# Segment 0 of a segmented memory attention: more projection work between the output rounds, output weights in smaller loads, value rows stored later

## The chip, the cores and the metric

The kernel runs on one core of a Trainium2 chip. The metric is the device time of one execution in microseconds (us), lower being better. A core has TensorE (PE in the profile; PEld is its weight load), VectorE (DVE), ScalarE (ACT), GpSimd (POOL) and SyncE (SP). DMA transfers are issued here from the queues of SP and ACT and run on the core's 16 DMA engines. "The profile" is one execution recorded by the hardware profiler; its page and the views of its trace are quoted below.

## What is computed

Two blocks follow each other on 2048 rows of 640 features. The first is attention with a recurrent memory: the rows are cut into 64 segments of 32, and each segment attends to itself and to 8 memory rows, which are the first 8 output rows of the segment before. The second is a dense layer with a squared ReLU.

```python
for s in range(n_seg):                         # 64 segments, one after another
    xs = x[:, s * seg_len:(s + 1) * seg_len, :]          # layernorm(x), 32 rows
    h = concatenate([mem, xs], axis=1)                   # 8 + 32 rows
    q = einsum('btd,dhe->bhte', h, Wq)                   # 32 heads of 128
    k = einsum('btd,dhe->bhte', h, Wk)
    v = einsum('btd,dhe->bhte', h, Wv)
    scores = where(mask, einsum('bhqe,bhke->bhqk', q, k) * scale, -1e9)
    o = einsum('bhqk,bhke->bhqe', softmax(scores), v)
    o = einsum('bhte,hed->btd', o, Wo)
    mem = o[:, :M, :]                                    # needed by the next segment
    outs.append(o[:, M:, :])
h = x + concatenate(outs)
out = h + relu(layernorm(h) @ w1 + b1)**2 @ w2 + b2
```

## The kernel before

Every matmul, transposes included, is issued by a helper, so all of them stand at line 114 or 118 of the profile; they are told apart by the tiles they write and read. The order of all instructions on all engines is written out by hand (`tc.manual_schedule`): each engine, and each DMA queue, works through its instructions in the order in which the Python code issues them, and waits in place where an operand or a buffer is not ready.

**Blocks and segments.** Four segments make a block of 128 rows; there are 16 blocks. A segment works on 32 rows: the 8 memory rows and the first 24 of its own rows. The last 8 rows of each segment do not touch the memory, so their q, k and v ("tails") are computed ahead, for a whole block at a time, as `tail_units`. A unit is four matmuls of 32 x 512 that run side by side in four column groups of the array; five units make one half (16 heads, 512 columns on 128 partitions) of a block's q, k or v. `tail_quarters` makes a quarter with matmuls 256 wide. Such units are put into the list `fill`, and `run(fill, n)` issues the next n of them at chosen places of `step`, the code of one segment.

**A segment (`step`).** q and k are projected; their results are copied out by ACT into row tiles (a pool of four buffers) and turned by DVE into qT and kT. Scores, softmax, v (copied by ACT into the tile v, lines 590 and 611), the products with the values (tile po) and 16 output rounds (`wo_rounds`, tile pw) follow. A round multiplies two heads of oT with wo in four matmuls of 320 columns. Rounds 0 to 7 use the even heads and rounds 8 to 15 the odd heads: round 8 the heads 1 and 17, round 9 the heads 3 and 19, round 12 the heads 9 and 25, and so on. After the last round DVE and ACT turn the 8 new memory rows into hT (`mem_to_hT`, lines 294 to 297), which the next segment's q needs. Fill issued behind the last round runs meanwhile.

**Segment 0** is special: its q, k and v are made in `start`, while the weights stream in (wv, wq, wk, then wo), together with those of block 0's tails. Its call of `step` has `ready` set.

**Values of the tails.** The value rows of a block's tails lie in row order; the product needs them in another order. So they are stored to a buffer in DRAM (vt_d, line 363) and gathered back into vt4 (`tails_v_in`, four DMAs, line 417). For block 0 the two stores are issued from ACT's queue in `start`; the gather for segment 0 (rows of which every fourth is used) comes from ACT's queue, and that for segments 1 to 3 from SP's queue, before the k stream. For blocks 1 and up the rows are kept in SBUF space that is not needed yet ("parked": parts of hnT0, ht0, oTts, vt4s, hT4, the tile v of segment 1, an xn tile) and stored in batches at the start of segments 1, 2 and 3 (`soon`, `stores`, last kept first). When no parked space is left, a row tile is used and stored at once.

**Loads on SP.** `load_wo` loads wo in eight DMAs: two of eight heads (the even heads), then odd heads in loads of 4, 4, 2, 2, 2 and 2 heads. Behind them stand the load of x for block 1 (line 139), the four gathers and, in segment 0, four loads of tail rows (line 148).

**Instruction padding.** PE's instructions are counted (`issued`), and `align` splits some 512-wide projections of the q and k of a segment into two of 256 (`halved`), so that the count at a chosen place of the segment falls on a multiple of 256.

Of the kernel before, what the change touches and what calls it, by code (L numbers as in the profile page):

```python
# [12 lines left out]
BF16 = mybir.dt.bfloat16  # L13
# [3 lines left out]
def kernel(  # L17
# [16 lines left out]
    nc = tc.nc  # L34
    _, S, D = A_x.shape
# [70 lines left out]

    ctx.enter_context(tc.manual_schedule(engines=None))

    issued, halved = [0], [0]
    BLOCK, AHEAD, PLACE = 256, 65, 34  # L110

    def matmul(*a, **k):
# [45 lines left out]

    def load_wo():
        wov = A_Wo.rearrange("h e d -> e h d")  # L160
        for h0, k in ((0, 8), (16, 8), (1, 4), (17, 4), (9, 2), (25, 2), (13, 2), (29, 2)):
            hs = slice(h0, h0 + 2 * k - 1, 2)
            nc.sync.dma_start(out=wo[:, hs, :], in_=wov[:, hs, :])  # L163

# [63 lines left out]
    def proj(w, by, lhs, n, ps, c0, c1):  # L228

        if by == "columns":  # L230
            wr = w[:].rearrange("p (c g j n k e) -> p c n k g j e", c=DC, g=G, n=2, j=4, k=4)
        elif by == "half":
            wr = w[:].rearrange("p (c k j n e) -> p c n k j e", c=DC, k=G, n=2, j=4)
        else:
            wr = w[:].rearrange("p (c k n f) -> p c n k f", c=DC, k=G, n=2)
        for c in range(c0, c1):
            for k in range(4):
                r = slice(32 * k, 32 * k + 32)
                if c and by == "columns" and halved[0]:
                    halved[0] -= 1  # L240
                    for u in range(2):
                        matmul(ps[r, u * 256:(u + 1) * 256], lhsT=lhs(c), rhs=wr[:, c, n, k, u * 2:u * 2 + 2],
                               start=False, stop=(c == DC - 1 and u == 1))
                    continue
                matmul(ps[r, :], lhsT=lhs(c), rhs=wr[:, c, n, k], start=(c == 0), stop=(c == DC - 1))

    def mmtile():
        return mm.tile([128, 512], F32, tag="mm", name="ps")
# [103 lines left out]
        return [unit(cs) for cs in ((0, 1), (2, 3), (4,))]  # L352

    def tail_out(b, which, n, ps):
        kept = which == "v" and 0 < b and len(parked) > 0
        row = parked.pop(0)() if kept else spare.pop(0) if spare else rowtile()[:]
        if which == "v" and b == 2:
            nc.vector.tensor_copy(out=row, in_=ps)
        else:
            evac_row(which, row, ps)  # L360
        if which == "v":
            def store(eng=nc.sync):
                eng.dma_start(out=vt_d[b, 2 * n:2 * n + 2].rearrange("j r f -> r j f"),
                              in_=row.rearrange("r (j f) -> r j f", j=2))
            if kept:
                stores.append(store)
            else:
                store(nc.sync if b else nc.scalar)
            return
        if n == 0:  # L370
            tails.setdefault(b, {})[which] = s2.tile([128, H, 32], BF16, tag=which + "Tt", name=which + "Tt")
        dst = tails[b][which]
        late.append(lambda: flip(row, dst, n))
# [30 lines left out]
        if "k" in which:  # L404
            nc.gpsimd.tensor_copy(out=kT[:, h0:h1, SEG:NK], in_=k)

    vt4s, stores = {}, []
    vt_d = dram.tile([NB, 4, 128, 2 * E], BF16)

    def tails_v_in(b, eng, s0=0, s1=4):  # L410
# [49 lines left out]
    def step(b, sp, v=None):  # L460
# [178 lines left out]
        wo_rounds(main, pw, 6, 8)  # L639
        if ready:  # L640
            tokens_sum()
        run(fill, 2 if ready else 1)
        wo_rounds(main, pw, 8, 12)
        if ready:
            run(fill, len(fill) - 6)
        wo_rounds(main, pw, 12, 16)

        if not ready:
            tokens_sum()
# [27 lines left out]
            tails_in((s + 1) // 4, (s + 1) % 4)  # L677
        run(mid, 2)
        o = wo_out(pw)
        run(fill, 100)  # L680
        if s > 1:
            store_main(o, s - 2)
        if last:
# [107 lines left out]
    def start():  # L791

        v = s2.tile([128, EG], BF16, tag="v", name="v")
        vs.append(s2.tile([128, EG], BF16, tag="v", name="v"))
        hT4s[1] = s2.tile([128, DC, 4, SEG], BF16, tag="hT4", name="hT4")
        park(hT4s[1][:, 0:4].rearrange("p c s t -> p (c s t)"))
        for u in range(2):
            park(vs[0][:, 512 * u:512 * u + 512])
        parked.append(lambda: s1.tile([128, D], BF16, tag="xn", name="vrow")[:, 0:512])
        main = lambda c: hT4s[0][:, c, 0, :]  # L800
        units = []

        def stream(which, w, dst, k=0):
            pa = pop.tile([128, 4, 512], F32, tag="po", name="pa")
            for c in range(DC):
                if which == "v" and c == DC - 1:
                    run(units, k)
                for n in range(2):
                    proj(w, "half" if which == "v" else "columns", main, n, pa[:, n, :], c, c + 1)
                for n in range(2):  # L810
                    proj(w, "order" if which == "v" else "columns", lambda c: tail_rows(0, c), n, pa[:, 2 + n, :], c, c + 1)
                if c < DC - 1:
                    run(units, k)
                    run(late, 100)
                if which == "q" and c == 1:
                    ln_stats(("t", 2))
                    ln_norm(("t", 2))
            for n in range(2):
                if which == "v":
                    nc.scalar.copy(out=v[:, n * 512:(n + 1) * 512], in_=pa[:, n, :])  # L820
                else:
                    row = rowtile()[:]
                    evac_row(which, row, pa[:, n, :])
                    flip(row, dst, n)
                    tail_out(0, which, n, pa[:, 2 + n, :])
                    late.pop()()
                    tails_in(0, 0, which, n * 16, (n + 1) * 16)
            if which == "v":
                for n in range(2):
                    tail_out(0, which, n, pa[:, 2 + n, :])  # L830

        ahead = [tail_units(1, "v"), tail_units(2, "v", (mmtile, lambda: chn.tile([128, 512], F32, tag="ch", name="pc")))]
        units += [a[n * DC + c] for c in range(DC) for a in ahead for n in range(2)]
        stream("v", wv, None, 4)
        ln_stats(("t", 1))
        ln_norm(("t", 1))
        units += tail_units(3, "v")
        units.insert(8, lambda: ln_transpose(("t", 1))())
        units.insert(11, lambda: None)
        units.insert(12, lambda: None)  # L840
        for b in (4, 5, 6):
            units += tail_units(b, "v")
        run(units, 6)
        load_tail_rows(2)
        load_w(wk, A_Wk)
        load_wo()
        load_x(1)
        stream("q", wq, qT, 7)
        for n in range(2):
            spread(n)  # L850
        units.append(lambda: ln_transpose(("t", 2))())
        units += tail_units(7, "v") + tail_units(1, "q") + tail_units(8, "v")
        run(units, 15)
        tails_v_in(0, nc.scalar, 0, 1)
        tails_v_in(0, nc.sync, 1, 4)
        stream("k", wk, kT, 6)
        units += tail_units(1, "k")
        run(units, 100)
        return v
# [13 lines left out]
    for b in (9, 10, 11, 12):  # L873
        parts = tail_units(b, "v")
        halves += [parts[:DC], parts[DC:]]
    del halves[-1], halves[4]
    quarters = [(11, "v", 0, 0), (11, "v", 0, 1)] + [(12, "v", 1, u) for u in range(2)]
    quarters += [(b, "v", n, u) for b in range(13, NB) for n in range(2) for u in range(2)]
    for b in range(NB):
        for sp in range(4):  # L880
            run(soon, 1)
            if sp == 2 and b + 2 < NB:
                load_x(b + 2)
            if b == 0:
                for h in range((3, 1, 1, 1)[sp]):
                    fill += halves.pop(0)
                if sp:
                    fill += tail_quarters(*quarters.pop(0))
                if sp < 3:
                    soon.append(lambda n=(8, 5, 5)[sp]: [stores.pop()() for _ in range(min(len(stores), n))])  # L890
                if sp == 1:
                    late.append(lambda: ln_stats(("t", 3)))
                    mid.append(lambda: ln_norm(("t", 3)))
                if sp == 2:
                    ln_turn(("t", 3))
                    late.append(lambda: ln_stats(1))
                    mid.append(lambda: ln_norm(1))
                if sp == 3:
                    ln_turn(1)
                    spare += [hnT0[:, c, :] for c in range(2)]  # L900
            elif b < NB - 1:
                if sp == 0:
                    fill += tail_units(b + 1, "q")[0:DC] + tail_quarters(b + 1, "q", 1, 0)
                if sp == 1:
                    parts = tail_units(b + 1, "k")
                    fill += tail_quarters(b + 1, "q", 1, 1) + parts[0:DC]
                if sp == 2:
                    fill += parts[DC:]
                    if quarters:
                        fill += tail_quarters(*quarters.pop(0))  # L910
# [141 lines left out]
```

## Time and profile before

| | |
|---|---|
| Time, median of 3 runs | 952.49 us (950.98 to 954.1) |
| The profiled execution | 952.75 us |
| Its span, first to last instruction | 950.9 us |
| TensorE busy | 927.1 us (97%), 25883 matmuls |
| VectorE, ScalarE, GpSimd busy | 704.2 us (74%), 546.0 us (57%), 256.7 us (27%) |
| DMA | 56.74 MB; the 16 engines are busy about all the time up to 60 us, and 10% of it or less in the long middle |
| Mean granted clock of TensorE | 0.998 |
| Chain that ended last | PE 92%, DMA 3%, DVE 2% |
| Segment 0 | about 49.8 to 63 us; a segment of block 0 after it takes about 11.8 us |

A share of busy time is a mean over stages with different limits. The first 60 us are the stage in which the weights come in; the middle is 63 segments in a chain; the dense block is the end. The change is at the border of the first stage and the second, so the table's shares say little of it, and the views that follow look at 50 to 70 us.

### The profile page before, as it was taken

To read this page: it belongs to the slowest core of one execution; us is meant where nothing else is said; L and a number is where in the kernel's file an instruction comes from. 1 tells how busy PE (TensorE), PEld (TensorE's weight loads), DVE (VectorE), ACT (ScalarE), POOL (GpSimd) and SP (SyncE) were. 2 spreads that over 40 slices of the span, in tenths; PEclk is the share of its full clock that TensorE was granted. 3 is DMA by queue.
4 is the path that set the end of the run, shared out by engine and by line. 5 is a ranking of instruction groups with operands and counts; after the bars stand their busy time and mean duration, and the time that the engine had idled before them with its cause. 6 is when DMAs were issued, how large, how long until landed. Compare 5 with 4: busy or idle time off the path is not lost.

```text
span 950.9 us, 57556 instructions
## 1 busy us (share of the span) xinstructions
PE 927.1 (97%) x25883; PEld 571.7 (60%) x25883; DVE 704.2 (74%) x2136; ACT 546.0 (57%) x1342; POOL 256.7 (27%) x798
## 2 busy tenths in 40 slices
PE   6989999999999999999999999999999998999998
PEld 2555665676566656666666566666666555555555
DVE  3268888888888888888888888888788888566632
ACT  3546666666666666666666666666566655523321
POOL 1012222222222222222222222222222233254200
PEclk9999999999999999999999999999999999999999
DMA  9973200101010101010101010101010111643220
GB/s 359 399 245 91 45 24 20 24 19 24 19 24 14 29 13 31 12 32 9 34 9 35 8 34 9 35 9 32 10 33 11 52 43 21 208 105 90 90 56 29
DMA packets 60710, 56.74 MB, mean 60 GB/s; under 512 B 27560, under 2 KB 56624, under 8 KB 58544
## 3 DMA queue, kind: packets, MB, share of 16 engines
q1 hardware_dynamic: 59776, 52.74, 18.5%
q8 instruction: 202, 3.31, 1.5%
q14 instruction: 44, 0.36, 0.1%
q10 hardware_dynamic: 688, 0.33, 0.1%
HBM read 38.37 MB, written 9.44 MB: 50 GB/s over the span
## 4 chain that ended last, share of the span: by engine, by line
PE 92%; DMA 3%; DVE 2%; ACT 1%; SPq 1%; issue 1%; POOL 0%; ACTq 0%; DVEq 0%
PE ps L114 62%; PE pw L114 16%; PE y L114 6%; PE po L114 5%; DMA vt_d<-row 1%; PE sm L114 1%; DMA wo<-in_A_Wo_dram 1%; SPq L163 1%; DMA vt<-vt_d 1%; PE pa L114 1%; DVE wk L975 0%; DVE lnst L170 0%; DMA xt<-in_A_x_dram 0%; ACT otc L295 0%; DVE otr L294 0%
## 5 line engine op out<-in xcount | busy, mean ns | idle before, releaser
L114 PEld LDWEIGHTS <-hT 128*32 128x32 bf16 x8358 | 220.3, 96 | 134.0 <-DVE hT L297 9.3
L114 PE MATMUL pw<-wo,oT 128*32 128x320 bf16 x4224 | 180.3, 301 | 3.5 <-DMA wo<-in_A_Wo_dram 3.2
L114 PE MATMUL ps<-wv,hT 128*32 128x512 bf16 x2520 | 177.4, 380 | 0.0
L114 PE MATMUL ps<-wq,hT 128*32 128x512 bf16 (+1 forms) x3143 | 160.2, 338 | 3.8 <-DVE hT L297 3.8
L114 PE MATMUL ps<-wk,hT 128*32 128x512 bf16 (+1 forms) x2575 | 159.2, 375 | 0.1
L114 PEld LDWEIGHTS <-oT 128*32 128x32 bf16 x4224 | 97.5, 96 | 58.5 <-DVE oT L252 20.2
L655 POOL TENSOR_TENSOR pkt<-ek,rk 128x64 bf16<-128x64 bf16 x64 | 19.2, 300 | 413.4 <-DVE rk L653 413.4
L261 ACT ACTIVATE row<-ps 128x512 bf16<-128x512 f32 (+1 forms) x170 | 94.0, 562 | 15.3 <-PE ps L114 11.9
L266 DVE STREAM_TRANSPOSE qT<-row 128x512 bf16<-128x512 bf16 x128 | 89.9, 702 | 9.7 <-ACT row L261 5.6
L974 ACT ACTIVATE wv<-ps,b1f 128x512 bf16<-128x512 f32 (+1 forms) x56 | 37.5, 672 | 67.4 <-PE ps L114 66.5
L443 ACT CAST oT<-po 128x512 bf16<-128x512 f32 x128 | 74.8, 587 | 0.0
L295 ACT COPY otc<-otr 64x40 f32<-64x40 f32 x126 | 28.0, 223 | 68.5 <-DVE otr L294 68.0
L454 POOL COPY qz<-qT 128x96 bf16<-128x96 bf16 x126 | 33.3, 265 | 115.4 <-DVE mx L505 58.2
L114 PEld LDWEIGHTS <-hTt 128*32 128x32 bf16 x1660 | 46.2, 98 | 29.8 <-issue 1.8
L114 PE MATMUL y<-wq,wk 128*128 128x320 bf16 x448 | 61.2, 300 | 0.2 <-DVE wk L975 0.2
L114 PEld LDWEIGHTS <-v 32*128 32x128 bf16 x4064 | 42.0, 91 | 32.0 <-issue 17.6
L263 ACT CAST row<-ps 128x512 bf16<-128x512 f32 (+1 forms) x111 | 60.2, 558 | 1.7 <-PE ps L114 0.9
L629 DVE TENSOR_REDUCE zk<-ek 128x8 f32<-128x320 bf16 x64 | 31.1, 486 | 38.1 <-ACT ek L628 38.1
L486 ACT CAST row<-ps 128x256 bf16<-128x256 f32 x126 | 40.7, 375 | 30.9 <-PE ps L114 30.9
L611 ACT CAST v<-ps 128x512 bf16<-128x512 f32 x63 | 36.9, 585 | 29.9 <-PE ps L114 29.9
L266 DVE STREAM_TRANSPOSE kT<-row 128x512 bf16<-128x512 bf16 x65 | 45.8, 705 | 10.1 <-ACT row L263 6.5
L114 PEld LDWEIGHTS <-wk 128*128 128x128 bf16 x448 | 40.5, 97 | 20.4 <-issue 5.0
(113 smaller groups left out, 1623.2 us busy)
## 6 DMA issues: line engine op xcount, KB each, us to landing
wv<-in_A_Wv_dram SPq DMA_DIRECT2D x5, 1024.0 KB
wq<-in_A_Wq_dram SPq DMA_DIRECT2D x5, 1024.0 KB
wk<-in_A_Wk_dram SPq DMA_DIRECT2D x5, 1024.0 KB
vt<-vt_d SPq DMA_DIRECT2D x60, 64.0 KB
xt<-in_A_x_dram SPq DMA_DIRECT2D x18, 160.0 KB
wo<-in_A_Wo_dram SPq DMA_DIRECT2D x2, 1280.0 KB
wq<-in_B_w_dram SPq DMA_DIRECT2D x1, 2080.0 KB
o_all<-o SPq DMA_DIRECT2D x128, 15.0 KB
```

The lines of the kernel that those rows point to most:

```text
L114: nc.tensor.matmul(*a, **k)
L261: nc.scalar.mul(out=row, in_=ps, mul=scale)
L263: nc.scalar.copy(out=row, in_=ps)
L266: nc.vector.transpose(out=dst[:, n * 16:(n + 1) * 16, 0:32], in_=row.rearrange("p (h e) -> p h e", e=32))
L295: nc.scalar.copy(out=tc_[:, a], in_=tr[64:128, a, :, 0:M])
L443: nc.scalar.copy(out=oTg[:, n, :, :, M:NK], in_=po[:, :, n * 128:(n + 1) * 128].rearrange("p g (j q) -> p g j q", q=32))
L454: nc.gpsimd.tensor_copy(out=d.rearrange("p a (j f) -> p a j f", j=3)[:, :, :, 0:M], in_=src[:, :, 0:3, :])
L486: nc.scalar.copy(out=row[:, u * 256:(u + 1) * 256], in_=ps[:, u * 256:(u + 1) * 256])
L611: nc.scalar.copy(out=v[:, 512:1024], in_=ps1[:])
L629: nc.vector.tensor_reduce(out=zk[:], in_=ek[:], op=ALU.add, axis=AX.X)
L655: nc.gpsimd.tensor_tensor(out=pkt[:], in0=ek[:, :, SEG:NK], in1=rk[:].unsqueeze(2).to_broadcast([128, HG, TL]), op=ALU.mult)
L974: nc.scalar.activation(out=r[:, 0:w], in_=ps[:, 0:w], func=ACT.Relu, bias=b1f[:, fc:fc + 1], scale=1.0)
```

## The change

- In segment 0 `fill` holds five halves, 25 units, instead of three halves, 15 units. The rounds 8 to 13 are issued in pairs, with 3, 5 and 4 units behind the pairs; 6 units remain behind the last round, with every matmul but those of the first chunk split in two (`split`).
- The odd heads of wo are loaded two at a time, in the order in which the rounds use them. There are ten loads of wo.
- Of block 0's value rows, every fourth is stored in `start` from ACT's queue, which is all that segment 0's gather reads. The rows themselves stay in parked space (one more xt tile is parked), and the full store is issued from SP's queue in segment 0, behind rounds 12 and 13 and their fill. The gather for segments 1 to 3 and the load of x for block 1 follow there; they stood in `start` before.
- The two halves that moved into segment 0 were four quarters in later segments: one in each of segments 1, 2 and 3, and one that makes the list of quarters one block shorter, so that block 13 has none.

```diff
-    issued, halved = [0], [0]
+    issued, halved, split = [0], [0], [False]
...
-        for h0, k in ((0, 8), (16, 8), (1, 4), (17, 4), (9, 2), (25, 2), (13, 2), (29, 2)):
+        for h0, k in ((0, 8), (16, 8), (1, 2), (17, 2), (5, 2), (21, 2), (9, 2), (25, 2), (13, 2), (29, 2)):
...
-                if c and by == "columns" and halved[0]:
-                    halved[0] -= 1
+                rhs = wr[:, c, n, k]
+                if c and (split[0] or by == "columns" and halved[0]):
+                    halved[0] -= 0 if split[0] else 1
+                    f = rhs.shape[1] // 2
                     for u in range(2):
-                        matmul(ps[r, u * 256:(u + 1) * 256], lhsT=lhs(c), rhs=wr[:, c, n, k, u * 2:u * 2 + 2],
+                        matmul(ps[r, u * 256:(u + 1) * 256], lhsT=lhs(c), rhs=rhs[:, u * f:(u + 1) * f],
...
-        kept = which == "v" and 0 < b and len(parked) > 0
+        kept = which == "v" and len(parked) > 0
...
-            if kept:
+            if b == 0:
+                first.append(store)
+                nc.scalar.dma_start(out=vt_d[0, 2 * n:2 * n + 2].rearrange("j (r s) f -> s r j f", s=4)[0],
+                                    in_=row[0:128:4].rearrange("r (j f) -> r j f", j=2))
+            elif kept:
                 stores.append(store)
             else:
-                store(nc.sync if b else nc.scalar)
+                store()
...
-        run(fill, 2 if ready else 1)
-        wo_rounds(main, pw, 8, 12)
-        if ready:
-            run(fill, len(fill) - 6)
-        wo_rounds(main, pw, 12, 16)
+            for h, k in ((8, 3), (10, 5), (12, 4)):
+                wo_rounds(main, pw, h, h + 2)
+                run(fill, k)
+            for f in first:
+                f()
+            tails_v_in(0, nc.sync, 1, 4)
+            load_x(1)
+        else:
+            run(fill, 1)
+            wo_rounds(main, pw, 8, 14)
+        wo_rounds(main, pw, 14, 16)
...
         o = wo_out(pw)
+        split[0] = ready
         run(fill, 100)
+        split[0] = False
...
+        parked.append(lambda: s2.tile([128, D], BF16, tag="xt", name="vrow")[:, 0:512])
...
         load_wo()
-        load_x(1)
...
         tails_v_in(0, nc.scalar, 0, 1)
-        tails_v_in(0, nc.sync, 1, 4)
...
-    del halves[-1], halves[4]
-    quarters = [(11, "v", 0, 0), (11, "v", 0, 1)] + [(12, "v", 1, u) for u in range(2)]
-    quarters += [(b, "v", n, u) for b in range(13, NB) for n in range(2) for u in range(2)]
+    quarters = [(b, "v", n, u) for b in range(13, NB) for n in range(2) for u in range(2)]
...
-                for h in range((3, 1, 1, 1)[sp]):
+                for h in range((5, 1, 1, 1)[sp]):
                     fill += halves.pop(0)
-                if sp:
-                    fill += tail_quarters(*quarters.pop(0))
```

More of the change, by code (lines that the diff above doesn't have):

```diff
@@ L238, in proj @@
                 r = slice(32 * k, 32 * k + 32)
-                if c and by == "columns" and halved[0]:
-                    halved[0] -= 1
+                rhs = wr[:, c, n, k]
+                if c and (split[0] or by == "columns" and halved[0]):
+                    halved[0] -= 0 if split[0] else 1
+                    f = rhs.shape[1] // 2
                     for u in range(2):
-                        matmul(ps[r, u * 256:(u + 1) * 256], lhsT=lhs(c), rhs=wr[:, c, n, k, u * 2:u * 2 + 2],
+                        matmul(ps[r, u * 256:(u + 1) * 256], lhsT=lhs(c), rhs=rhs[:, u * f:(u + 1) * f],
                                start=False, stop=(c == DC - 1 and u == 1))
                     continue
-                matmul(ps[r, :], lhsT=lhs(c), rhs=wr[:, c, n, k], start=(c == 0), stop=(c == DC - 1))
+                matmul(ps[r, :], lhsT=lhs(c), rhs=rhs, start=(c == 0), stop=(c == DC - 1))
     def mmtile():
@@ L405, in tails_in @@
             nc.gpsimd.tensor_copy(out=kT[:, h0:h1, SEG:NK], in_=k)
-    vt4s, stores = {}, []
+    vt4s, stores, first = {}, [], []
     vt_d = dram.tile([NB, 4, 128, 2 * E], BF16)
```

## The prediction

> **What bounds the kernel now.** The page first: TensorE is busy 97% of the span, and its share of the chain that ended last is 92%, so work taken from TensorE shortens the kernel one for one where TensorE is busy. The waits of TensorE came next: 3.2 us of its idle time, in 5 pieces, ends on the output weights (wo). The timeline of TensorE puts all five into segment 0 (columns: start, length, engine, line, operation, and in brackets the idle time before and what ended it):
>
> ```profile
> 54.99 0.32 PE L114 MATMUL pw<-wo,oT 128*32 128x320 bf16 x2
> 56.78 0.72 PE L114 MATMUL pw<-wo,oT 128*32 128x320 bf16 x14 [1.48 <-DMA wo<-in_A_Wo_dram]
> 57.68 0.31 PE L114 MATMUL pw<-wo,oT 128*32 128x320 bf16 x2 [0.18 <-DMA wo<-in_A_Wo_dram]
> 58.54 0.45 PE L114 MATMUL pw<-wo,oT 128*32 128x320 bf16 x6 [0.55 <-DMA wo<-in_A_Wo_dram]
> 59.39 0.31 PE L114 MATMUL pw<-wo,oT 128*32 128x320 bf16 x2 [0.40 <-DMA wo<-in_A_Wo_dram]
> 60.33 0.53 PE L114 MATMUL pw<-wo,oT 128*32 128x320 bf16 x6 [0.62 <-DMA wo<-in_A_Wo_dram]
> 60.48 2.94 PE L114 MATMUL ps<-wv,hTt 128*32 128x512 bf16 x24
> 62.95 1.89 PE L114 MATMUL ps<-wq,hT 128*32 128x512 bf16 x20
> ```
>
> The reader should see that rounds 8 to 15 wait for one load after another, and that the last six fill units (24 matmuls) only come behind them. The windows view, cut at the clock's steps, gives TensorE's busy time (first number after the length) and the granted clock (third number from the end):
>
> ```profile
> 53.74:57.15 3.41, 1.94 (x60) 1.09 (x55) 2.81 (x6) 0.73 (x2) 0.00 (x0) 1.00 1.07 363
> 57.15:60.56 3.41, 1.66 (x28) 0.54 (x23) 0.08 (x1) 0.00 (x0) 0.00 (x0) 1.00 0.77 258
> 60.56:63.97 3.41, 3.41 (x40) 2.76 (x35) 1.82 (x7) 1.97 (x5) 1.57 (x4) 0.50 0.22 73
> ```
>
> So a stretch with 1.66 us of work was followed by 3.41 us at half clock. The chain of waits shows the last load landing at 51.69 + 8.60 = 60.29. The last two views are the timelines of SP's queue and of ACT:
>
> ```profile
> 38.13 14.42 SPq L163 DMA_DIRECT2D wo<-in_A_Wo_dram  x8
> 52.65 0.74 SPq L139 DMA_DIRECT2D xt<-in_A_x_dram  x1
> 53.43 4.83 SPq L417 DMA_DIRECT2D vt<-vt_d  x4
> 58.56 3.12 SPq L148 DMA_DIRECT2D ht<-in_A_x_dram  x4
> 64.06 0.37 SPq L363 DMA_DIRECT2D vt_d<-row  x1
> 64.48 0.47 SPq L363 DMA_DIRECT2D vt_d<-vrow  x1
> 64.99 1.03 SPq L363 DMA_DIRECT2D vt_d<-v  x2
> 96.03 2.67 SPq L417 DMA_DIRECT2D vt<-vt_d  x4
> ```
>
> ```profile
> 69.39 0.58 ACT L590 CAST v<-ps 128x512 bf16<-128x512 f32 x1 [0.18 <-PE ps L114]
> ```
>
> The loads at lines 417 and 148 start as earlier wo loads land: a transfer is issued only when the eighth before it has landed, since eight semaphores go round. The two stores from v landed at 67.00 and 67.53 by the trace's completion events, and the copy at 69.39, which overwrites the same buffer, waited only for TensorE.
>
> **Step 1: the last output weight.** Three quarters of block 0's two value stores leave the stretch before it, 196,608 bytes. By bytes at the 415 GB/s of 10 to 20 us this is 0.47 us. By landings: the four weight chunks around the stores took from 26.67 to 38.11, 11.44 us, where an undisturbed chunk took 2.48 (38.11 to 40.59) and the row load among them 0.39 by its bytes; the rest is 1.1 us, three quarters of it 0.85. I take 0.8, as the landings hold the cost of 512-byte runs. Two-head loads in order of use don't change the last byte: an 8-head load took 3.58 us (49.49 to 53.07), a 2-head load 0.86 to 0.93. The last load lands at 60.3 - 0.8 = 59.5, earlier ones 0.9 apart: 58.6, 57.7, 56.8, 55.9. The two extra issues on SP are hidden by that backlog; without it they would cost some 0.5 us each.
>
> **Step 2: fill among the rounds.** Twenty 512-wide matmuls take 1.08 us (65.62 to 66.70), so a unit of four is 0.216. Ahead of the last round stood 9 units and now stand 19; the extra ten are 2.16 us inside waits of 3.23 us, which hide them. The last round again ends 0.58 after the last load, at 60.1. The next segment needs hT, ready 1.10 after that round (61.96 against 60.86), so at 61.2. The six units behind the round take 1.3 us from 59.7 at full clock, as the stretch before is now filled, and are done by 61.0. Segment 1 starts at 61.2, not 62.95: 1.75 us. Before, another 1.02 us of it ran at half clock, worth 0.51. Together 2.26 us ahead.
>
> **Step 3: what leaves later segments.** Four groups of twenty 256-wide matmuls are gone, one each in segments 1, 2, 3 and in block 13. The matmuls from 73.97 to 75.38 are sixteen wide and twenty narrow: 1.41 - 16 x 0.054 = 0.55 each, 2.2 us in all, TensorE being busy there. Another 168 matmuls are split in two (20 in segment 0 by the flag, and by the padding 128 in segments 1 to 4 and 20 in block 13). Two halves take 2 x 0.0275 against 0.054, so the cost is between nothing and 168 x 1 ns = 0.2 us; I take nothing, as the narrow ones stream without a gap in that row.
>
> **Step 4: a new wait in segment 1.** On SP now stand, in order: ten wo loads, four tail-row loads, two row stores, block 0's two full stores, the four gathers, x(1), two row stores, two parked rows, then v's second and first half. By the round of eight, block 0's second full store waits for the last wo load, so it is issued at 59.5. Alone a store lands in 1.9 us (64.06 to 65.93). Behind four row loads (0.21 each, landings 62.98 to 63.61) and three stores (0.53 each, their spacing), with its own 0.53, it lands in up to 3.0. I take 2.5, nearer the backlog: 62.0. The first gather waits for it. Four gathers take 2.7 us of issue (96.03 to 98.70), x(1) 0.55, five stores 0.53 each: v's first half is issued at 62.0 + 2.7 + 0.55 + 2.65 = 67.9 and lands 2.0 later, at 69.9. ACT's copy of segment 1's values into v must wait for that. TensorE would want it by 69.39 - 2.26 = 67.1. The copy takes 0.58, and the value matmuls behind it, at 70.17 before, start at 70.5. On ACT the second exponential is queued behind the copy, on TensorE everything, so the delay is carried on: the 2.26 us are gone and 0.35 more. Bounds of this link: landing at 69.2 to 70.4 by the store's 1.9 to 3.0, and later by 1.6 if the v store takes 3.6, as the one issued at 67.14 did (landed 70.72).
>
> The gathers, moved past the tail rows and stores, land about 66.1; values want them at 67.9, so 1.8 us hide them. x(1), moved the same way, lands near 67 and is read in segment 2, past 82. ACT keeps its two issues of block 0, smaller ones; POOL's queue issues no DMA here and is not touched. Block 12's rows are now read by fill near 96, and their transpose landed at 84.6.
>
> **Sum.** Profiled execution 952.75 = span 950.9 and 1.85 outside it; the median of runs is 952.49, 0.26 less. 952.75 - 2.2 + 0.35 = **950.9**. Its own range, by the bounds of step 4, is 950.2 to 953.0.
>
> **Rivals.** *The chain on SP is short enough.* If v's store lands by 67.1, segment 0's gain stays: 952.75 - 2.2 - 2.26 = 948.3. For it: issue and transfer overlap, and the fast DMA engines finish wo 2 us before the slow ones (landings 58.25 to 60.28). Against: the gathers wait for all engines. By the Trainium skill (DMA: Bandwidth & Descriptors, SWDGE vs HWDGE vs iDMA), a sequencer's time to initiate a transfer is usually small beside the transfer; by that rule this case would hold. The rows here disagree: 0.53 us of issue for each 128 KB store.
>
> *The clock falls in the new stall.* TensorE would stand from 67.9 to 70.5. A window of 3.41 us that holds 2.6 us of it has 0.8 us of work, less than the 1.66 that brought half clock; windows run free of the kernel, so about half of their positions hold enough. Price 3.41 / 2 = 1.7: 952.6. By the Trainium skill (TensorE: Matmul & The Clock Gate, What's actually happening) the clock drops after a whole idle window; by that this stall is too short, and the first case stays. The row at 57.15 dropped with half a window of work, so I keep this case.
>
> *Slower: a lagging DMA engine on both links.* Stores issued at 67.14, 67.67 and 68.21 landed 3.58, 3.25 and 3.03 us later, in place of 2.0. If block 0's store and v's store both meet that, 1.6 us each, the copy starts at 73.1 and values at 73.7, 3.55 us late, and a stall of 5.8 us holds a whole window, so the half clock is sure: 952.75 - 2.2 + 3.55 + 1.7 = 955.8. It decides from a v landing past 72.9. Against it: a lag hits three stores in nine.
>
> **How the numbers follow.** Forecast 0.42, short chain 0.24, clock 0.18, lag 0.16. The range takes in the first three: 948.0 to 953.8, and leaves the lag, 0.16, outside. A measurement of this kernel can tell about 0.3% (2.9 us) from no change. Faster by more is the short chain and the best end of the forecast, 0.25; slower by more the lag and a little, 0.18; within it 0.57.
>
> **What would show it.** Right: wo waits of TensorE under 1 us and its last round done near 60.1; clock 1.00 from 60 to 64; a TensorE gap of some 2.6 us in segment 1 ended by ACT's copy of v (line 596 now), that copy idle until a store from v lands near 69.9; segments 1 to 3 0.55 shorter each. Wrong: no such gap (then 948.3), or half clock near 70 to 74 (then 952.6 or more), or a last wo load still at 60.3.

## The result and the profile after

| | changed kernel | kernel before, same chip | ratio, 95% interval |
|---|---|---|---|
| time, median | 955.77 us (953.60 to 958.57, 12 runs) | 953.08 us (949.88 to 954.80, 12 runs) | 1.0032 (1.0021 to 1.0044) |
| profiled execution | 954.77 us, span 953.0 | 952.75 us, span 950.9 | |

The changed kernel is slower by about 0.3%; the forecast was 950.9 us, faster than before by 1.85. The views that follow answer to those of the prediction.

First the chain of waits in segment 1 (start, length, what). SPq is SP's queue, and line 365 is the store to vt_d.

```profile
68.37 0.53 SPq L365
...
68.94 3.26 DMA vt_d<-v
...
72.27 0.59 ACT v L596
...
72.91 0.32 PE po L114 x15
```

The last store from v is issued at 68.94 and lands 3.26 us later. ACT's copy into v waits for that, and the value products on TensorE wait for the copy. The timelines of ACT and TensorE say the same from their sides:

```profile
72.27 0.58 ACT L596 CAST v<-ps 128x512 bf16<-128x512 f32 x1 [4.36 <-DMA vt_d<-v]
72.75 0.30 ACT L514 ACTIVATE em<-sm,mx 128x40 bf16<-128x40 f32 x1
```

```profile
60.65 0.45 PE L114 MATMUL pw<-wo,oT 128*32 128x320 bf16 x6 [0.41 <-DMA wo<-in_A_Wo_dram]
60.80 1.60 PE L114 MATMUL ps<-wv,hTt 128*32 128x256 bf16 x44
62.25 1.27 PE L114 MATMUL ps<-wq,hT 128*32 128x512 bf16 x36
...
68.56 0.41 PE L114 MATMUL ps<-wv,hT 128*32 128x512 bf16 x4
72.91 0.27 PE L114 MATMUL po<-pTm,v 32*128 32x8 bf16 x16 [3.94 <-ACT v L596]
```

TensorE stands for 3.94 us where it did not stand before. The upper three lines are the end of segment 0: the output rounds are done just behind 60.65, and segment 1 starts at 62.25, not at 61.2 as predicted. SP's queue shows why v's stores come so late:

```profile
61.15 0.46 SPq L365 DMA_DIRECT2D vt_d<-ht  x1
63.16 2.63 SPq L423 DMA_DIRECT2D vt<-vt_d  x4
65.83 0.45 SPq L139 DMA_DIRECT2D xt<-in_A_x_dram  x1
66.39 0.88 SPq L365 DMA_DIRECT2D vt_d<-row  x2
67.31 1.01 SPq L365 DMA_DIRECT2D vt_d<-vrow  x2
68.37 1.65 SPq L365 DMA_DIRECT2D vt_d<-v  x2
```

The line at 61.15 is block 0's second full store. The gathers (line 423) wait until it has landed, and everything below stands behind them. Last the windows view at the steps of the clock (busy TensorE after the length; granted clock third from the end):

```profile
67.68:71.09 3.41, 1.30 (x52) 0.69 (x44) 1.15 (x7) 0.23 (x2) 0.00 (x0) 1.00 0.83 238
71.09:74.50 3.41, 1.59 (x36) 0.79 (x40) 1.14 (x6) 1.11 (x4) 0.00 (x0) 0.50 0.56 158
74.50:77.92 3.42, 3.42 (x104) 1.96 (x100) 1.70 (x4) 0.98 (x3) 0.00 (x0) 0.50 0.02 5
77.92:81.33 3.41, 3.10 (x84) 1.94 (x80) 2.30 (x9) 1.45 (x4) 0.99 (x3) 1.00 0.02 5
```

The half clock that stood at 60.56 before is gone from segment 0, but two windows of it now follow the new stall. From segment 1's first scores to segment 2's the kernel takes 17.75 us, where it took 11.91.

### The profile page after: what moved, and what is told of

It reads as the page before. It is cut to its first block, busy times and chain, and to the rows that moved or that the text cites. A ratio compares the mean times of both kernels' runs of the same rounds, so it can differ in the third digit from the quotient of the medians.

```text
span 953.0 us, 57809 instructions
## 1 busy us (share of the span) xinstructions
PE 927.1 (97%) x26002; PEld 570.4 (60%) x26011; DVE 700.8 (74%) x2136; ACT 545.3 (57%) x1340; POOL 257.2 (27%) x798
## 4 chain that ended last, share of the span: by engine, by line
PE 91%; DMA 6%; DVE 1%; ACT 1%; issue 0%; SPq 0%; DVEq 0%; ACTq 0%
PE ps L114 62%; PE pw L114 16%; PE y L114 6%; PE po L114 5%; DMA wo<-in_A_Wo_dram 2%; DMA wq<-in_A_Wq_dram 2%; DMA wk<-in_A_Wk_dram 1%; PE sm L114 1%; DMA wv<-in_A_Wv_dram 1%; ACT otc L297 0%; DMA vt_d<-v 0%; DVE otr L296 0%; DVE hT L299 0%; SPq L365 0%; DVE qT L268 0%
## 5 line engine op out<-in xcount | busy, mean ns | idle before, releaser
L114 PE MATMUL pw<-wo,oT 128*32 128x320 bf16 x4224 | 182.3, 302 | 1.6 <-DMA wo<-in_A_Wo_dram 1.3
L114 PE MATMUL ps<-wq,hT 128*32 128x256 bf16 (+1 forms) x3211 | 159.6, 333 | 5.0 <-DVE hT L299 5.0
L297 ACT COPY otc<-otr 64x40 f32<-64x40 f32 x126 | 28.0, 223 | 67.2 <-DVE otr L296 66.7
```

What stands on the lines that cost most here:

```text
L114: nc.tensor.matmul(*a, **k)
L297: nc.scalar.copy(out=tc_[:, a], in_=tr[64:128, a, :, 0:M])
```

## The experiments

Each run lies beside runs of the kernel before on the same chip. In the first group these had a median of 951.17 us, in the second (f) 949.31, in the third (g1 to g4) 952.58, so ratios are compared, not times. The main question is whether v's place in SP's queue is the cause, and what the rest of the change does.

**v's stores first (e1).** The changed kernel with the two stores of v ahead of block 0's full stores; nothing else is different.

```diff
-            for f in first:
+            for f in [stores.pop(-3), stores.pop(-3)] + first:
...
-                    soon.append(lambda n=(8, 5, 5)[sp]: [stores.pop()() for _ in range(min(len(stores), n))])
+                    soon.append(lambda n=(6, 5, 5)[sp]: [stores.pop()() for _ in range(min(len(stores), n))])
```

> The changed kernel, with the two rows parked in v stored on SP ahead of block 0's full stores, so that they land near 63 us and not at 72. Theory (ACT's copy into v waits for v's store, which stands behind the gathers on SP): the 3.94 us gap of TensorE in segment 1 is gone, the clock stays 1.00 from 60 to 80 us, the step from the scores of segment 1 to those of segment 2 falls from 17.75 to about 12.0 us, and the time to 950.0 (955.8 - 5.8) or 951.9 (953.1 less the 1.16 us by which segment 1 began earlier). Rival (the gathers are late, v only looks guilty): they are issued a little later still, so a gap over 2 us stays, now ended by a gather, and the time stays over 954. Rival (the time is lost after segment 1, by thin fill and splits): the time stays over 954 without a gap.

Measured: 950.21 us, ratio 0.9994 (0.9984 to 1.0005). In its timelines of SP's queue and of ACT the stores go out at 60.38, and the copy waits only for TensorE:

```profile
60.38 1.53 SPq L365 DMA_DIRECT2D vt_d<-v  x2
```

```profile
68.63 0.59 ACT L596 CAST v<-ps 128x512 bf16<-128x512 f32 x1 [0.22 <-PE ps L114]
```

There is no half clock, and the step from segment 1 to 2 is 11.89 us. So the place of these two stores makes the difference between slower and level. The gathers go out 1.3 us later than in the changed kernel, at 64.49, and land by 69.51. The last of the value products that read them starts at 69.56: no wait for them shows, but no room is left either.

**The fill part alone (e2) and the store part alone (e3, and again as g3).** e2 has the change's fill, rounds and wo loads, with stores, gathers and x(1) of before; e3 has the fill, rounds and wo loads of before, with block 0's full stores, gathers and x(1) issued ahead of rounds 14 and 15.

```diff
 e2, against the changed kernel
-        kept = which == "v" and len(parked) > 0
+        kept = which == "v" and 0 < b and len(parked) > 0
...
-            for f in first:
-                f()
-            tails_v_in(0, nc.sync, 1, 4)
-            load_x(1)
...
 e3, against the kernel before
-        wo_rounds(main, pw, 12, 16)
+        wo_rounds(main, pw, 12, 14)
+        if ready:
+            for f in first:
+                f()
+            tails_v_in(0, nc.sync, 1, 4)
+            load_x(1)
+        wo_rounds(main, pw, 14, 16)
```

> The changed kernel's fill, rounds and wo loads, with block 0's full stores, the gathers and the load of x where they stood before the change. Theory: no gap on v, since v's stores are issued near 64 as before the change; time 951 to 952. If the smaller stores of block 0 ahead of wo paid their 0.65 us, the last wo load lands 0.65 later here than in the run with v's rows first; if not, they are equal within 0.3. Rival (the fill between the rounds or the split matmuls lose the time): 955 or more.

> The kernel before with the store part of the change alone: every fourth row of block 0 stored early, full stores, gathers and x behind round 13 on SP, 15 fill units as before. Theory: ACT's copy into v waits until about 72 us, TensorE stands some 2 us in segment 1 and the clock halves behind it: 956 to 958. Rival (the fill is to blame): 953.

> The store part alone on the fill of before, again. Its first profile held the stall (3.71 us) and two windows of half clock, and was 4.5 us behind the first profile of before over segments 2 to 10, while its median was no slower. Theory (the stall is always there, and the rest of that kernel saved the instruction stalls that the profile of before had): gap of 3.4 to 4 us again, segments 11 to the last 597 to 599 us, median within 0.3% of before. Rival (stall in some executions only): a gap under 2.5 us in this profile, or a median 0.3% or more slower now.

Measured: e2 949.81 us, 0.9987 (0.9975 to 0.9998). e3 951.48 us, 1.0006 (0.9995 to 1.0016), and again 954.40 us, 1.0017 (1.0005 to 1.0030). The fill part alone is a small gain: 10 of its 11 runs have a mean clock of 1.000, where 28 of the 29 runs of before beside it lie below that. Its last wo load lands at 61.51, where e1's lands at 61.10; the 0.41 between them lies between the two cases of the expectation, so it doesn't settle whether the smaller stores save anything (step 1 below). The store part alone has the stall in both profiles, 3.71 and 2.12 us:

```profile
72.47 0.27 PE L114 MATMUL po<-pTm,v 32*128 32x8 bf16 x16 [3.71 <-ACT v L594]
```

Both runs missed their expectations: e3 was to take 956 to 958 us, or 953 by its rival, and g3 was to have a gap of 3.4 to 4 us again. The cost in the medians is under 2 us, against a stall of 2 to 4, and the parts do not add up to the whole (-0.13% and +0.06 or +0.17%, against +0.32 and, below, +0.45%). Where the rest of e3's stall is won back was not found. Stalls of TensorE with no wait shown, in segments 11 to 61, move by up to 4 us from one execution to the next (e3 597.62 us for that stretch, g3 601.75), so its profiles can't tell.

**TensorE kept busy (e4, f2).** 128 matmuls whose result nothing reads, ahead of segment 1's first value products: in e4 into a tile of its own, in f2 into columns 320 to 511 of po.

```diff
 f2 (e4: idle[r, 0:256] of idle = mmtile(), rhs=wv[:, 0:256])
+        if s == 1:
+            for i in range(128):
+                r = slice(32 * (i % 4), 32 * (i % 4) + 32)
+                matmul(po[r, i % 4, 320:512], lhsT=lhs(0), rhs=wv[:, 0:192], start=True, stop=True)
```

> The changed kernel, with 128 matmuls of 256 columns ahead of segment 1's first value products; nothing reads their result. They are 3.4 us of work inside the stall of 3.94. Theory (half clock behind the stall is worth some 1.9 us of the 5.84): the copy of v still waits until about 72, the clock stays 1.00, time 953.9. Rival (half clock costs nothing there, as other engines set the pace): 955.8.

e4 priced nothing: its tile took over the buffer that the copy into v reads, so the matmuls waited for the copy and ran behind it; 958.16 us, 1.0069 (1.0055 to 1.0083).

> The changed kernel unchanged, on the chip and in the minutes of the other experiments, with a second profile. Theory (the stall before ACT's copy into v is in every execution, some 3 to 4 us, and one or two windows of half clock follow, 1.7 us each): 954.5 to 957 where the kernel before is at 951 to 952, and the second profile shows a TensorE gap over 3 us on that copy again. Rival (the long landing of v's store is an accident of some executions, so that only part of the loss is always there): a gap of 2.0 to 2.6 us in the second profile, no half clock or one window, and a median of 952.5 to 954.

> The changed kernel with 128 matmuls 192 columns wide (2.6 us of TensorE at full clock) into columns of segment 1's po that nothing reads, ahead of that segment's first value products, so that TensorE works through the stall; unlike in the run before they share no buffer with what the copy into v reads. Theory (half clock follows from the idle time and costs half of what it covers): the value products start no later than in the changed kernel (72.9 give or take 0.5), the clock stays at 1.00 from 68 to 80, and the step from segment 1's scores to segment 2's falls from 17.75 to 15.7 to 16.1; the median lies 1.5 to 2 us under the changed kernel's. Rival (half clock comes from something else, or hides behind another wait): half clock at 71 to 78 stays, or the step stays within 0.5 us of 17.75.

Measured: the changed kernel again (f1) 953.21 us, 1.0045 (1.0033 to 1.0058), with a gap of 3.62 us and half clock from 71.25 to 78.08, much as in its first profile. f2 951.91 us, 1.0031 (1.0020 to 1.0043). f2's timeline, and its windows at the clock's steps:

```profile
68.37 1.67 PE L114 MATMUL po<-wv,hT 128*32 128x192 bf16 x72
70.30 1.34 PE L114 MATMUL po<-wv,hT 128*32 128x192 bf16 x56 [0.26 <-issue]
72.31 0.26 PE L114 MATMUL po<-pTm,v 32*128 32x8 bf16 x16 [0.67 <-ACT v L596]
```

```profile
67.86:71.28 3.42, 3.16 (x164) 2.85 (x156) 0.59 (x4) 0.00 (x0) 0.00 (x0) 1.00 0.67 195
71.28:74.69 3.41, 2.74 (x140) 1.68 (x132) 1.87 (x8) 1.46 (x4) 0.00 (x0) 1.00 0.48 136
```

The value products start at 72.31 with or without the idle matmuls (f1: 72.34), the clock stays full, and the step to segment 2 is 15.61 us where f1 has 17.79. So the half clock costs 2.2 us in a profile, and 1.3 us between the medians.

**v's stores three places earlier (g4).** Right behind x(1), ahead of two row stores and two parked rows, but still behind block 0's stores and the gathers.

```diff
             load_x(1)
+            for u in range(2):
+                stores.pop(-3)()
...
-                    soon.append(lambda n=(8, 5, 5)[sp]: [stores.pop()() for _ in range(min(len(stores), n))])
+                    soon.append(lambda n=(6, 5, 5)[sp]: [stores.pop()() for _ in range(min(len(stores), n))])
```

> The changed kernel, with v's two stores issued right behind x(1), ahead of the two row stores and the two parked rows (three places of the queue earlier than in the changed kernel, still behind block 0's stores and the gathers). Theory (the wait is the place of v's stores in SP's queue, and the packet of instructions at 67.7 to 68.7 on top): issued near 65.9 and 66.4, they are nearly down when the packet comes, land at 67.9 to 68.6, and the gap before the value products is 0 to 0.6 us, with no half clock; median 949.5 to 951 where the kernel before is at 949.3 to 951.2. Rival (the gathers in front hold the engines, whatever the place): landing past 69.5, gap over 1.2 us and a median 951 or more.

Measured: 954.35 us, 1.0021 (1.0011 to 1.0031). The theory missed, the rival held. Chain of waits:

```profile
66.98 4.39 DMA vt_d<-v
...
71.44 0.59 ACT v L596
...
72.08 0.30 PE po L114 x20
```

Issued 1.96 us earlier than in the changed kernel, the last store lands only 0.83 earlier. The first of the two takes 2.95 us, where a store takes 2.0. The load x(1) ahead of it takes 3.06 and the last gather 3.02, half a microsecond more than the 2.50 and 2.62 that they took in e3. So what stands in front of v's stores holds them up as well, as the rival had it; the rest of the 4.39 is the next point.

**The packets of instructions (g2, h1).** In the trace's packet records the instructions come as packets of 16,384 bytes, which in this stretch hold one DMA engine for 0.9 to 1.8 us each. One came at 68.67 in the changed kernel. Its page counts 203 of these packets, and 26,011 matmuls with as many weight loads: 52,022 instructions, or 203 times 256. By the Trainium skill (Advanced Engine Details and Errata, ISA Cache) a cache line is 16 KB, 256 instructions, and the trace agrees. g2 drops the 44 padding splits of segment 1, with which those of segments 2 and 3 and 13 of segment 4 fall away too, 128 in all. h1 splits 40 more fill matmuls of segment 0 (80 instructions, not the 144 of its expectation) and gives segment 1 35 splits in place of 44.

```diff
 g2
-        halved[0] = short // 2 if short <= 128 else 0
+        halved[0] = short // 2 if short <= 128 and s > 1 else 0
 h1
+            split[0] = True
             for h, k in ((8, 3), (10, 5), (12, 4)):
...
-        halved[0] = short // 2 if short <= 128 else 0
+        halved[0] = 35 if s == 1 else short // 2 if short <= 128 else 0
```

> The changed kernel without the padding splits in segments 1 to 4 (256 TensorE instructions fewer), which moves the 16 KB packets of instructions against the stores: in the run without padding on the other stores they came at 65.0 and 71.5, and none between. Theory (v's store lands 3.3 us after its issue instead of 2.0, or is issued 0.5 to 1.1 us late, because such a packet holds one DMA engine for about a microsecond at 67.7 to 68.7): with no packet between 66 and 70, each store of the row lands 1.8 to 2.2 us after its issue, v's second one near 70.5, and the gap before the value products is 1.8 to 2.5 us. Rival (stores in a row lag by themselves, by their bytes): landing 3 us or more after issue and a gap over 3.2 us all the same. The segments themselves get stalls of 1 us or so, as without padding before; the whole time tells nothing here.

> The changed kernel with 72 more fill matmuls of segment 0 split in two (144 TensorE instructions more, which by the runs cost TensorE nearly nothing), so that the next packets of 256 instructions come about half a block earlier: near 66 instead of 67.8 to 68.7, and the one after it not before the stall has ended. Theory (the long landing of v's stores is the packet that falls into their transfer): the stores issued from 66 to 66.9 are hit now, the ones of v, issued at 68.1 to 69.0, land 2.0 to 2.5 us after their issue, the second one at 70.6 to 71.3, and the gap before the value products is 2.3 to 3.0 us. Rival (v's stores lag because of what stands in front of them in the DMA engines: gathers, x(1) and four stores): they land 3.2 us or more after issue and the gap stays at 3.6 to 4.0. The whole time tells little, since later segments lose the place of their packets.

Neither moved the packet as far as meant: it came at 69.13 in g2 and at 67.84 in h1. Each ran once, in 958.59 and 954.20 us, with before at 953.70 beside them; nothing is read from these times. Still the two tell the cases apart, with the other profiles (us; v's last store, and the packet nearest to it):

| kernel | store issued | packet starts | issue to landing |
|---|---|---|---|
| before; again (g1) | 65.54; 64.94 | 68.72; 67.23 | 1.99; 1.98 |
| e2; f3 | 67.09; 66.12 | 68.75; 68.39 | 1.98; 1.99 |
| e1; e4; f4 | 61.45; 69.73; 67.23 | 59.60; 68.06; 64.98 | 1.98; 2.09; 2.00 |
| h1 | 70.13 | 67.84 | 2.00 |
| f1; f2 | 69.46; 69.43 | 67.81; 67.67 | 2.16; 2.17 |
| changed kernel; g2 | 68.94; 68.70 | 68.67; 69.13 | 3.26; 3.24 |
| e3; g3; g4 | 67.79; 67.46; 66.98 | 68.17; 68.16; 68.93 | 3.97; 3.62; 4.39 |

Where a packet starts from 0.3 us before the store's issue to 0.7 behind it, the store lands 3.2 to 4.0 us after its issue; with one 1.65 us before it or 1.66 behind it, about 2. (g4's came 1.95 behind its store, which was late already.) But a store that escapes gains nothing: in h1's chain of waits one ahead of v's is held in SP's queue instead.

```profile
67.94 1.63 SPq L365
...
69.62 0.47 SPq L365
...
70.13 2.00 DMA vt_d<-v
```

A store that takes 0.5 us to issue takes 1.63 just after the packet, and v's last store lands at 72.13, where the changed kernel's lands at 72.20. In these two the packet seems to cost its microsecond in the one form or the other. h1 also shows a second buffer in the same trap, in ACT's timeline: a row tile that segment 1 needs is still being stored.

```profile
70.45 0.65 ACT L492 CAST row<-ps 128x256 bf16<-128x256 f32 x2 [3.77 <-DMA vt_d<-row]
```

The completion events say more than the table. A store lands in sixteen parts. In each of the fifteen profiles there is a transfer whose last part comes 0.7 to 2.3 us behind its fifteenth, and 1.04 to 1.33 us behind the end of a packet of instructions. In the changed kernel the packet ends at 69.61. The store issued at 66.80 has its fifteenth part at 69.33 and its last at 70.82, the last parts of the stores behind it follow 0.2 to 0.4 us apart, and v's last store is the fourth behind it, at 72.19. In f4, with the store order of before, the packets start at 64.98 and 71.54, and the six stores issued from 66.72 to 69.37 land in 1.96 to 2.02 us each.

That the packet delays the stores rests on this timing in fifteen profiles; no run had the changed kernel's stall with the packet gone. Nor is all of the lag the packet's: in g3 x(1) and the first row store, which took 3.36 and 3.17 us to land, were down before the packet began at 68.16.

**Fill and splits (f3, f4), on e2.** f3 puts the one fill unit that stands ahead of round 8 in segments 1 to 3 behind the last round; f4 drops the padding splits there.

```diff
 f3
-            run(fill, 1)
+            if s > 3:
+                run(fill, 1)
 f4 (align is called with the segment plus the block: 5 for segment 4)
-        halved[0] = short // 2 if short <= 128 else 0
+        halved[0] = short // 2 if short <= 128 and s > 4 else 0
```

> The run with the fill part alone (stores as before), and in segments 1 to 3 the one fill unit of four matmuls that stood before round 8 goes behind the last round with the other four. Theory (TensorE waits 0.31 us in those segments because the fill behind the last round covers 0.75 us of the 1.06 that the turn of the memory rows takes): the three gaps on hT shrink by a unit, 0.216, to 0.09 each, and the segments by as much, 0.65 in all; median 949.2 where the fill part alone was 949.8. Rival (the gap is set by something that moves along, as the exponential for the token sum on ACT ahead of it): gaps stay at 0.31.

> The run with the fill part alone (stores as before), without the padding splits of query and key projections in segments 1 to 3 (35 or 36 matmuls in each). Theory (a split costs TensorE some 5 ns): segments 1 to 3 each 0.17 to 0.2 shorter, 0.5 to 0.6 in all, if instruction fetch doesn't stall there; median 949.2 to 949.5. Rival 1 (a split costs nothing, as the prediction had it): steps between segments as in the fill part alone, 11.77 to 11.80. Rival 2 (the padding pays for itself): the missing instructions move the fetch into the segments and stalls of 0.1 to 1 us with no wait shown appear in them, and the steps are 11.8 to 12.8.

Measured: f3 948.13 us, 0.9990 (0.9981 to 0.9999); f4 950.15 us, 1.0011 (1.0003 to 1.0020). Segment 3 and the start of segment 4 in e2, then in f3, by TensorE's timeline:

```profile
95.58 0.46 PE L114 MATMUL pw<-wo,oT 128*32 128x320 bf16 x8
95.86 0.39 PE L114 MATMUL ps<-wv,ht 128*32 128x512 bf16 x4
96.08 1.27 PE L114 MATMUL pw<-wo,oT 128*32 128x320 bf16 x32
97.18 1.04 PE L114 MATMUL ps<-wv,ht 128*32 128x512 bf16 x16
98.52 1.27 PE L114 MATMUL ps<-wq,hT 128*32 128x512 bf16 x36 [0.30 <-DVE hT L299]
```

```profile
94.97 1.78 PE L114 MATMUL pw<-wo,oT 128*32 128x320 bf16 x40
96.57 1.25 PE L114 MATMUL ps<-wv,ht 128*32 128x512 bf16 x20
97.91 0.51 PE L114 MATMUL ps<-wq,hT 128*32 128x512 bf16 x8
```

The gap on hT shrinks to 0.09 as the theory had it, but no segment gets shorter: the steps from segment 2 to 3 and from 3 to 4 are 11.77 to 11.78 us in both, and that from 1 to 2 is 11.80 in e2 and 11.90 in f3. The forty round matmuls take 1.60 us by their starts in f3, and the same forty with the unit among them take 1.60 in e2 (95.58 to 97.18): ahead of round 8 the unit had covered a wait for oT. The idle time shown is also too small: from the start of the last fill to q are 1.34 us in e2, of which sixteen matmuls need 16 x 0.054 = 0.86, so a gap shown as 0.30 costs 0.48. In f4 q and k of segment 3 take 4.33 us from their first start to the scores, with 35 splits in e2 4.35: a split costs next to nothing. But without them the segments stall where nothing is waited for:

```profile
74.14 0.32 PE L114 MATMUL pw<-wo,oT 128*32 128x320 bf16 x4 [1.13 <-issue]
```

Another stall, 0.99 us on a transposing DMA, follows in segment 2. So the padding seems to pay for itself; that a stall comes from where the instructions fall is not shown.

**The kernel before again (g1).**

> The kernel before, for a second profile. From segment 11 to the last step between segments its first profile took 601.3 us, where the profiles of the changed kernel and of the experiments took 597.2 to 599.3; the excess are stalls of TensorE with no wait shown, in segments that fetch more instructions than the others. Theory (these stalls are an accident of one execution): 597 to 599.5 now. Rival (they belong to this kernel's layout of instructions, and every kernel with other counts saves 2 to 4 us of them): 600.5 or more.

Measured: 949.89 us, and 599.75 us for that stretch, between the two cases: neither held, and whether these stalls are an accident of an execution is not settled. This execution had no half clock in segment 0, and its segment 1 had its scores at 66.27, earlier than the changed kernel's 66.62.

## Why the prediction failed, step by step

The forecast was 952.75 less 2.2 (step 3) plus 0.35 (step 4), and both terms failed. The quarters were worth about 0.2 in all, and the wait in segment 1 cost 2.74 where 0.35 was allowed, with 2.2 of half clock behind it, which the sum put at nothing.

*Step 1* fell. The last wo load landed at 60.60, not 59.5. The smaller early stores save nothing that these profiles show. Step 1 read its 0.8 us off the weight chunks around the stores, whose stretch ended at 38.11 before; with the smaller stores it ends at 38.08 and 37.97 (e3, g3), without them at 38.11 and 37.99 (before, g1). The wo loads agree: in e3 and g3 the second lands at 53.19 and 52.86 and the last at 60.40 and 60.09, and in before and g1 at 53.07 and 52.91, and 60.28 and 60.24. The ten loads, which step 1 let cost nothing, seem to cost some tenths: with them the last wo load lands at 60.19 to 61.10 in eight profiles with the smaller stores, and at 60.74 to 61.51 in three without (e2, f3, f4). No run had the ten loads alone.

*Step 2* was right in its mechanism: rounds wait 1.3 us for wo in place of 3.2 (1.8 in e2), and the half clock of segment 0 is gone. That fits e2's small gain. Segment 1's scores come 1.16 us ahead, not 2.26; most of the missing 1.1 is the last wo load of step 1, 1.1 late. But the baseline was one execution with a half clock that before has in most executions, not in all (g1).

*Step 3* fell: four quarters were to save 0.55 us each, 2.2 in all. The step from segment 2 to 3, which nothing else disturbs, is 11.77 us in e2 and f1 against 11.81 before, so a quarter saved 0.04. Step 3 took TensorE as busy there and did not ask what the quarter covered. It covered the turn of the memory rows. Before, VectorE's timeline has the last pieces of hT here:

```profile
74.83 0.42 DVE L297 TENSOR_TENSOR hT<-otr,otc 64x40 bf16<-64x40 f32 x2
```

They were written by 75.25, and the next q, which reads them, began at 75.38: only some 0.13 us could be won. The gap that takes the quarter's place costs 0.48. That splits cost next to nothing was right.

*Step 4* named the right wait and mis-sized it: +0.35 us was to be lost, and the value products start at 72.91, 2.74 later than before (70.17) and 2.41 later than its 70.5. The first gather went out at 63.16 and not at 62.0. Block 0's second store, which it waits for, was issued 1.65 late, at 61.15: 1.1 of that is the last wo load, and 0.55 the store ahead of it, whose issue took 1.08 in place of 0.47; it then landed in 1.96 and not in 2.5. The queue from first gather to v's last store took 5.78 (5.9 predicted), and that store landed in 3.26 in place of 2.0. So 1.16 - 0.12 + 1.26, and 0.11 from landing to value products, make the 2.41.

*The rivals.* The short chain fell: ten issues of 0.37 to 0.66 us each, with 0.04 to 0.11 between them, make up that 5.78. By the Trainium skill (DMA: Bandwidth & Descriptors, Issuing engines are not separate DMA queues) a sequencer's time to initiate a transfer is usually small beside the transfer; for one store the trace agrees (0.53 us of issue, 2.0 to land), but ten in a row make up more than the landing of any store here. The half clock came, at 2.2 us instead of 1.7. The slower case, 955.8, was nearest, but that it lies within 0.1 us of the median is luck: it still took off 2.2 for the quarters, its two lags of 1.6 were one of 1.26, its half clock was too cheap, and the profile's later segments happened to be 2.0 us shorter. The lag hit the second of its two links; the first was late by the wo load and a long issue. I gave it 0.16 because three stores in nine lagged before; but the stores that lag are mostly ones in flight with a packet of instructions, which starts at 67.2 to 69.1 us in fourteen of fifteen profiles, and my own forecast put v's store there.

The terms against the profile: 950.9 + 2.41 (values) + 2.2 (clock) + 4 x 0.51 (quarters) = 957.6, measured 954.77. Of the 2.8 left, 2.0 are the stretch from segment 11 to 61 (601.30 before, 599.29 after), which varies by execution; 0.8 stays unattributed.

Of the runs, f3 and e2, the fill part without the moved stores, are faster than the kernel before, by 0.10% (0.01 to 0.19) and 0.13% (0.02 to 0.25), intervals that only just lie clear of no change.

## What to carry to other kernels

Before a store is moved down a queue, list every buffer that is stored behind it and who overwrites that buffer next; two of these stores placed first were worth 0.4 to 0.5% of this kernel. Before work is taken from a busy engine, look for the wait that starts where it ended: filler that covers a chain is not cost. And price a landing by the stores issued at that time, not by the mean over all.

## What was not expected of the hardware

A packet of 256 instructions holds one DMA engine for 0.88 to 1.78 us here. By their timing, stores in flight with it land up to 4.7 us after their issue (e3) in place of 2.0; the last part of the first one hit comes 1.04 to 1.33 us behind the packet's end. Or a later store's issue takes 1.0 to 2.3 us in place of 0.5. This coincidence stands in fifteen profiles; that the one causes the other was not shown by a run.

The half clock follows half an idle window, and ends later than it begins. Cut at the clock's own steps of 3.41 us, which stand elsewhere in each execution, fifteen profiles show it, from 45 to 82 us, after every one of ten windows with 0.12 to 1.68 us of work, and after none with 1.80 or more (1.68 is from segment 0 of g3, 1.80 from that of g1). Once there it stayed for another window after 1.59, 2.32, 2.40 and 2.66 us of work, and ended after 2.85 or more. So before falls into it or not by where the windows happen to lie, and a stall of the changed kernel's kind brings one window of it (e4, g4, h1) or two (f1, g2) by the same chance. By the Trainium skill (TensorE: Matmul & The Clock Gate, What's actually happening) the clock drops after a whole idle window; these rows differ, and they decide.
